# Attention scores as three float32r products of two halves, on the two halves of TensorE's rows

## The chip, the cores and the metric

The kernel runs on one core of one Trainium2 chip. The metric is device time in microseconds (us) of one execution, the median over the runs. The engines are TensorE (PE for its matmuls, PEld for its weight loads), VectorE (DVE), ScalarE (ACT) and GpSimd (POOL); the DMA transfers of this kernel are issued from SyncE's queue (SP).

## The reference, cut to what matters

Attention over 8 batches with 8 heads, 576 tokens and 64 numbers a head, and a gated layer on what it gives:

```
scores = scale * q @ k.T                       # [8, 8, 576, 576]
keep   = scores >= max(scores, axis=-1) - tau
attn   = softmax(where(keep, scores, -1e9))
x      = (attn @ v), heads side by side        # [4608, 512]
out    = (sigmoid(x @ w_gate) * (x @ w_val)) @ w_out   # d_ff = 1536
```

All inputs are float32.

## The kernel before, in words

**Staging.** A program in two layers runs on one core. The attention layer goes through 32 visits, one for each batch and each pair of heads. A visit has nine tiles of 128 queries: four of the first head, four of the second, and one "leftover" tile with the last 64 queries of both heads (its names have an `l`). For a tile, `tile_steps` computes 128x576 scores into PSUM (buffer `s`, two banks of 288 columns, two buffers in turn, L609), DVE takes the maximum (L616), the threshold is made from it (L625), ACT takes the exponential into SBUF (`p`, L630), and DVE zeroes what is below the threshold and sums (L633). A group of one or two tiles is then normalised on POOL (L667), transposed on TensorE (`tp`, L678; `lk` for the last 64 keys, L691), copied out (L640, L641), and multiplied with v (`av`, L714).

The second layer has products with 512 moving columns (`m` for the two input weights, L774; `o` for the output weights, L817). Three blocks of 512 tokens, batches 0 to 2, go this way during the attention. The other six blocks run after the last visit, two at a time, as seven products in place of eight (L1016, L1081; `two_blocks`), with sums of weights (`sums`, L868) made on POOL before.

**How scores are computed.** For the first four visits (`plain_s`, batch 0) scores are float32 matmuls: the stationary operand has 128 rows, of which one head's are non-zero (the input `q0` holds q so), the moving operand is k of both heads, in two halves of 288 keys. In the other 28 visits each float32 number is a sum of two float32r numbers, hi and lo. ACT makes hi of k and q (L529, L531), POOL makes lo of k (L533), DVE lo of q (L536), each for both heads at once, 640 columns. Then DMAs within SBUF lay the halves out anew: for each head, `qd` holds hi of q in one half of the partitions and lo in the other (L546), and `kd` holds hi of k in both halves of the partitions, and lo of k in both (L550). A matmul with 128 rows then gives hi·hi + lo·hi, and a second one hi·lo + lo·lo; with two halves of the keys a tile takes four matmuls with 128 rows and 288 moving columns. The leftover tile of such a visit takes six, from the tiles `q2` and `k2` that were not laid out anew.

**What sets the order.** Every step is given to `plan.op` with an engine, a cost, a key (lower goes first) and the buffers that it reads and writes. `Plan.run` walks a clock with these costs and emits each engine's instructions in the order that it finds. Attention tiles have keys that count up over the visits (`first`); a visit's loads and splits come `LEAD` tiles ahead; conversions of the weights have keys from `CONV_IN` and `CONV_OUT`; `SHIFT` is added to the keys of the visits from batch 1 on; matmuls of the second layer have keys of 1e6 and up, so that they fill what attention leaves of TensorE. `SLOTS` says how many buffers a tag has. `THR_UNTIL` and `LK_UNTIL` say up to which key the threshold is made on POOL instead of DVE, and the copy of `lk` on ACT instead of DVE. `SUMS_IN` and `SUMS_OUT` say in which block the sums of weights are made. The buffers of `two_blocks` come, in part, from tags that attention uses.

Of the kernel before, what the change touches and what calls it, by code (L numbers as in the profile page):

```python
# [43 lines left out]
class Plan:  # L44
# [3 lines left out]
    IN_TURN = ("x", "xf", "kn", "qn", "vn", "k2", "q2", "kd", "qd", "vs", "p", "pt", "pl", "ptc")  # L48
# [151 lines left out]
    "kn": 1, "qn": 1, "vn": 1, "k2": 1, "q2": 1, "kd": 3, "qd": 3, "vs": 3,  # L200
# [3 lines left out]
LEAD = 3  # L204
# [7 lines left out]
EARLY = 16  # L212
# [4 lines left out]
NPS = 4  # L217
# [15 lines left out]
THR_FIRST, THR_UNTIL, LK_UNTIL = "POOL", 72, 72  # L233
# [11 lines left out]
SHIFT = 20  # L245
# [13 lines left out]
KD_COST = 1.2  # L259
# [3 lines left out]
SUMS_IN, SUMS_OUT, SUM_KEY = {1: (0,), 2: (1,)}, {0: (0,), 1: (1,)}, 400  # L263
# [25 lines left out]
def kernel(  # L289
# [3 lines left out]
    q0: bass.AP,  # L293
# [22 lines left out]
    B, NPAIR, P, SK = k.shape  # L316
# [15 lines left out]
    assert D == 64 and SL == 64 and SK == SM + 2 * SL and ND == NPAIR == NJ and B * SL == SM  # L332
# [152 lines left out]
    class Visit:  # L485


        def __init__(self, b, hp, kind, first):
            self.b, self.hp, self.kind, self.first = b, hp, kind, first

            self.plain_s = 4 * b + hp < NPS
            self.of_tiles = {}
            self.name = f"{b}_{hp}{kind}"
            self.c0, self.c1 = {"": (0, SM), "a": (0, SM // 2), "b": (SM // 2, SM)}[kind]
            g0, g1 = [(0, (0, 1)), (1, (0, 1))], [(0, (2, 3)), (1, (2, 3))]
            left = [(None, (NJ,))]
            self.groups = {"": g0[:1] + left + g1[:1] + g0[1:] + g1[1:], "a": g0, "b": left + g1}[kind]
            self.with_left = kind != "a"
# [4 lines left out]
        def prepare(self, lead):  # L503
            key, n = self.first - lead, self.name
            b, hp = self.b, self.hp
            self.xf = buf("xf", [P, S], F32, f"xf{n}")
            if self.plain_s:
                self.plain_scores(key, n)
            else:
                self.split_scores(key, n)  # L510
# [4 lines left out]
        def split_scores(self, key, n):  # L515
            b, hp = self.b, self.hp

            kn = buf("kn", [P, SK], F32, f"kn{n}")
            op("SP", 1.2, key - 4, lambda: nc.sync.dma_start(out=kn.ap, in_=k[b, hp]), writes=[kn])


            c0, c1 = self.c0, self.c1 + (2 * SL if self.with_left else 0)
            W, WM = c1 - c0, self.c1 - self.c0
            qn = buf("qn", [P, W], F32, f"qn{n}")
            op("SP", 1.2, key - 4, lambda: nc.sync.dma_start(out=qn.ap, in_=q[b, hp, :, c0:c1]), writes=[qn])


            k2 = self.k2 = buf("k2", [P, 2, SK + P], F32R, f"k2{n}")
            op("ACT", 0.73, key, lambda: nc.scalar.copy(k2.ap[:, 0, :SK], kn.ap), reads=[kn], writes=[(k2, 0)])  # L529
            q2 = self.q2 = buf("q2", [P, 2, W], F32R, f"q2{n}")  # L530
            op("ACT", act(W), key, lambda: nc.scalar.activation(q2.ap[:, 0], qn.ap, AF.Copy, scale=scale_t[:, 0:1]),  # L531
               reads=[qn], writes=[(q2, 0)])
            op("POOL", pool(SK), key, lambda: nc.gpsimd.tensor_tensor(  # L533
                out=k2.ap[:, 1, :SK], in0=kn.ap, in1=f32(k2.ap[:, 0, :SK]), op=ALU.subtract
            ), reads=[kn, (k2, 0)], writes=[(k2, 1)])
            op("DVE", 1.4 * W / 640, key, lambda: nc.vector.scalar_tensor_tensor(  # L536
                out=q2.ap[:, 1], in0=qn.ap, scalar=scale_t[:, 0:1], in1=f32(q2.ap[:, 0]), op0=ALU.mult, op1=ALU.subtract
            ), reads=[qn, (q2, 0)], writes=[(q2, 1)])
            self.WM = WM
            self.kd, self.qd = {}, {}  # L540
            for h in range(2):
                kd = self.kd[h] = buf("kd", [P, 2, SK], F32R, f"kd{n}_{h}")
                qd = self.qd[h] = buf("qd", [P, WM], F32R, f"qd{n}_{h}")
                own, other = slice(h * D, (h + 1) * D), slice((1 - h) * D, (2 - h) * D)
                for z, rows in enumerate((own, other)):
                    op("SP", 0.5, key + h, lambda qd=qd, rows=rows, own=own, z=z: nc.sync.dma_start(  # L546
                        out=f32(qd.ap[rows]), in_=f32(q2.ap[own, z, :WM])
                    ), reads=[(q2, z)], writes=[(qd, z)])
                for rows in (own, other):
                    op("SP", KD_COST, key + h, lambda kd=kd, rows=rows, own=own: nc.sync.dma_start(  # L550
                        out=f32(kd.ap[rows]), in_=f32(k2.ap[own, :, :SK])
                    ), reads=[k2], writes=[(kd, rows.start)])

        def plain_scores(self, key, n):
            b, hp, c0, c1 = self.b, self.hp, self.c0, self.c1
            WM = self.WM = c1 - c0
            kn = self.k1 = buf(("kn", "qn")[hp % 2], [P, SK], F32, f"kp{n}")
            op("SP", 1.2, key - 4, lambda: nc.sync.dma_start(out=kn.ap, in_=k[b, hp]), writes=[kn])
            W = 2 * WM + (2 * SL if self.with_left else 0)
            qn = self.q1 = buf("kd", [P, W], F32, f"qp{n}")  # L560

            heads = [(0,), (1,)] if n == "0_0" else [(0, 1)]
            for hs in heads:
                c = slice(hs[0] * WM, (hs[-1] + 1) * WM)
                op("SP", 0.9 * len(hs), key - 4, lambda hs=hs, c=c: nc.sync.dma_start(
                    out=qn.ap[:, c].rearrange("p (h c) -> p h c", h=len(hs)),
                    in_=q0[4 * b + hp, :, hs[0] : hs[-1] + 1, c0:c1],
                ), writes=[(qn, h) for h in hs])
            if self.with_left:
                op("SP", 0.3, key - 4, lambda: nc.sync.dma_start(out=qn.ap[:, 2 * WM :], in_=q[b, hp, :, SM:]),  # L570
                   writes=[(qn, 2)])
            if len(heads) == 1:
                op("ACT", act(W), key, lambda: nc.scalar.activation(qn.ap, qn.ap, AF.Copy, scale=scale_t[:, 0:1]), writes=[qn])
                return
            for i, c in enumerate((slice(0, WM), slice(WM, 2 * WM), slice(2 * WM, W))):
                op("ACT", act(c.stop - c.start), key, lambda c=c: nc.scalar.activation(
                    qn.ap[:, c], qn.ap[:, c], AF.Copy, scale=scale_t[:, 0:1]
                ), writes=[(qn, i)])

    def tile_steps(vis, g, i, key):  # L580
# [8 lines left out]
        cols = None if h is None else slice(qt * P - vis.c0, (qt + 1) * P - vis.c0)  # L589
        if vis.plain_s:  # L590
            at = 2 * vis.WM if h is None else h * vis.WM + cols.start
            steps = [(lambda: vis.q1.ap[:, at : at + P], lambda c: vis.k1.ap[:, c])]
            reads = [(vis.q1, 2 if h is None else h), vis.k1]
        elif h is None:
            steps = [
                (lambda a=a: vis.q2.ap[:, a, vis.WM :], lambda c, z=z: vis.k2.ap[:, z, c])
                for a, z in ((0, 0), (0, 1), (1, 0))
            ]
            reads = [vis.q2, vis.k2]
        else:  # L600
            steps = [
                (lambda: vis.qd[h].ap[:, cols], lambda c, z=z: vis.kd[h].ap[:, z, c]) for z in range(2)
            ]
            reads = [vis.qd[h], vis.kd[h]]

        def scores():
            for m, (st, mv) in enumerate(steps):
                for c in range(2):
                    nc.tensor.matmul(  # L609
                        s.ap[:, c, :HALF], st(), mv(slice(k0 + c * HALF, k0 + (c + 1) * HALF)),  # L610
                        start=m == 0, stop=m == len(steps) - 1,
                    )

        op("PE", 0.98 if vis.plain_s else len(steps) * 2 * mm(HALF), key, scores, reads=reads, writes=[s], also=[g.p])
# [480 lines left out]
    def two_blocks(k):  # L1095

        key = 400 + k
        tags = ["x"] * 5 + ["vs"] * 2 + ["k2"] + ["kd"] * 3 + ["p"] * 3
        whole = lambda b: Part(b, lambda: b.ap)
        xt, j = {}, 0  # L1100
        for prod in SEVEN:
            xt[prod] = []
            for c in range(2):
                xt[prod].append(whole(buf(tags[j], [P, 2, SM], F32R, f"xs{k}_{prod}_{c}")))
                j += 1
# [111 lines left out]
    plan.run()  # L1217


_INS = ["q", "q0", "k", "v", "tau", "moe_w_gate", "moe_w_val", "moe_w_out"]  # L1220
_OUTS = [((512, 4608), "float32")]


# [73 lines left out]
```

## Time and profile before

| what | value |
|---|---|
| median of 3 runs | 1374.51 us (1374.49 to 1381.02) |
| the profiled execution's own time | 1375.02 us |
| its span, first to last instruction | 1373.2 us |
| mean granted TensorE clock | 0.995 |
| busy: PE, PEld, DVE | 1332.4, 1099.7, 982.3 us |
| busy: ACT, POOL | 708.8, 639.0 us |
| DMA | 317.70 MB, 231 GB/s |

The span and the profiled execution's own time differ by 1.8 us. Busy times are unions over a group of instructions; a matmul's record is longer than the step to the next one, since matmuls are pipelined, so the price of a tile of matmuls is read from the starts in the timeline: from its first start to the first start of what follows. A float32 matmul (`kp`,`qp` and `av`) has two records in the trace, a float32r matmul and a transpose one. L-numbers are lines of the kernel.

### The profile page before, as it was taken

Reading aid. Unit: us, or ns where it says so; the run is one execution under the profiler, and the core shown is the slowest. Engines: PE = TensorE matmul, PEld = TensorE weight load, DVE = VectorE, ACT = ScalarE, POOL = GpSimd, SP = SyncE. Lnnn points to the kernel's source line nnn. Section 1 sums busy time; section 2 is a strip of 40 time slices with the busy share of each in tenths; the row PEclk is TensorE's granted clock in tenths of the full one; section 3 lists DMA queues with packets and bytes.
Section 4 is the critical chain, followed back from the end, with each engine's and each line's share of the span. In section 5 each row is a group of like instructions: output and inputs, shape, how many; then the busy total and the mean of one; then the engine's idle time right before and its main releaser. Section 6 shows DMA issues by size and latency. Waiting matters only on the chain.

```text
span 1373.2 us, 23632 instructions
## 1 busy us (share of the span) xinstructions
PE 1332.4 (97%) x8276; PEld 1099.7 (80%) x8276; DVE 982.3 (72%) x2070; ACT 708.8 (52%) x1225; POOL 639.0 (47%) x681
## 2 busy tenths in 40 slices
PE   6888999999999999999999999999999999999998
PEld 5666888888788788888888887888888888888887
DVE  5898888777778787777878783456974569745584
ACT  5776766665566666566667663222532225322242
POOL 4888865884676685686787653011000110001100
PEclk9899999999999999999999999999999999999999
DMA  5769899888688779798879677766686566766664
GB/s 214 284 218 326 286 256 272 266 242 255 206 238 245 200 226 285 203 297 246 238 221 275 208 210 260 234 184 193 208 288 215 185 194 209 245 194 187 195 208 140
DMA packets 140292, 317.70 MB, mean 231 GB/s; under 512 B 22032, under 2 KB 49168, under 8 KB 140176
## 3 DMA queue, kind: packets, MB, share of 16 engines
q1 hardware_dynamic: 140032, 316.20, 75.0%
q8 instruction: 67, 1.10, 0.3%
q14 instruction: 49, 0.40, 0.1%
q10 hardware_dynamic: 144, 0.00, 0.0%
HBM read 210.24 MB, written 54.53 MB: 193 GB/s over the span
## 4 chain that ended last, share of the span: by engine, by line
PE 88%; DMA 4%; DVE 3%; issue 2%; POOL 2%; ACT 1%; SPq 0%; POOLq 0%; ACTq 0%; DVEq 0%
PE m L774 13%; PE qb L1016 11%; PE av L714 11%; PE s L609 10%; PE tp L678 7%; PE qc L1016 7%; PE qa L1016 7%; PE o L817 6%; PE rb L1081 5%; PE rc L1081 4%; PE ra L1081 4%; PE s_l L609 2%; DVE p L633 1%; PE tp_l L678 1%; PE lk L691 1%
## 5 line engine op out<-in xcount | busy, mean ns | idle before, releaser
L667 POOL TENSOR_SCALAR p<-p,zero_t,sm 128x576 f32<-128x576 f32 x256 | 215.1, 850 | 101.6 <-DVE sm L665 61.7
L616 DVE TENSOR_REDUCE st<-s 128x1 f32<-128x576 f32 x256 | 192.8, 754 | 84.0 <-PE s L609 82.6
L630 ACT ACTIVATE p<-s,st 128x576 f32<-128x576 f32 x256 | 190.5, 748 | 66.8 <-DVE st L616 56.3
L633 DVE SCALAR_TENSOR_TENSOR p<-s,st,p 128x576 f32<-128x576 f32 x256 | 206.4, 811 | 25.2 <-ACT p L630 19.0
L929 POOL TENSOR_TENSOR gA<-gA 128x512 f32<-128x512 f32 x18 | 24.2, 1343 | 417.1 <-DVE gA L995 417.1
L640 ACT COPY pt<-tp 128x512 f32<-128x512 f32 x256 | 148.6, 587 | 74.4 <-PE tp L678 73.4
L678 PE MATMUL tp<-ident,p 128*128 128x128 f32 x1024 | 157.0, 278 | 8.4 <-POOL p L667 8.1
L609 PE MATMUL s<-kd,qd 128*128 128x288 f32 x896 | 161.6, 305 | 3.5 <-DMA qd<-q 2.4
L774 PE MATMUL m<-x,wi 128*128 128x512 f32 x576 | 161.5, 405 | 0.0
L678 PEld LDWEIGHTS tp<-ident,p 128*128 128x128 f32 x1024 | 123.3, 142 | 34.6 <-POOL p L667 13.2
L609 PEld LDWEIGHTS s<-kd,qd 128*128 128x128 f32 x896 | 133.8, 189 | 14.4 <-DMA qd<-q 2.9
L714 PE MATMUL av<-pt,vs 128*64 128x256 f32 x1024 | 126.3, 385 | 0.7 <-ACT pt L640 0.7
L817 PE MATMUL o<-g,wo 128*128 128x512 f32 x432 | 120.1, 404 | 0.0
L953 DVE TENSOR_TENSOR qu<-qb,qp 128x512 f32<-128x512 f32 x72 | 49.8, 692 | 92.2 <-PE qb L1016 66.1
L774 PEld LDWEIGHTS m<-x,wi 128*128 128x128 f32 x576 | 98.8, 189 | 13.6
L1016 PE MATMUL qa<-xs_p,wa 128*128 128x512 f32 x432 | 109.6, 389 | 0.0
L714 PEld LDWEIGHTS av<-pt,vs 128*64 128x64 f32 x1024 | 68.4, 136 | 48.5 <-issue 7.7
L1016 PEld LDWEIGHTS qa<-xs_p,wa 128*128 128x128 f32 x432 | 81.1, 188 | 16.8
L817 PEld LDWEIGHTS o<-g,wo 128*128 128x128 f32 x432 | 74.5, 189 | 10.5
L921 ACT CAST gs_p<-gA 128x512 fp32r<-128x512 f32 x54 | 32.7, 620 | 77.4 <-DVE gA L995 41.5
L991 ACT ACTIVATE gA<-qa 128x512 f32<-128x512 f32 x18 | 10.8, 598 | 103.4 <-PE qa L1016 103.4
L640 ACT COPY xf<-av 128x256 f32<-128x256 f32 x64 | 25.6, 399 | 74.1 <-PE av L714 70.7
(151 smaller groups left out, 2687.5 us busy)
## 6 DMA issues: line engine op xcount, KB each, us to landing
kd<-k SPq DMA_DIRECT2D x112, 320.0 KB, 4.9
wi<-wid SPq DMA_DIRECT2D x48, 512.0 KB, 7.4
wo<-wod SPq DMA_DIRECT2D x36, 512.0 KB, 6.9
wa<-wid SPq DMA_DIRECT2D x36, 512.0 KB, 3.3
ws<-sid SPq DMA_DIRECT2D x36, 512.0 KB, 4.4
wt<-sid SPq DMA_DIRECT2D x36, 512.0 KB, 3.3
wo_p<-sod SPq DMA_DIRECT2D x36, 512.0 KB, 4.5
qd<-q SPq DMA_DIRECT2D x112, 128.0 KB, 3.4
```

Source lines behind the costliest of these rows:

```text
L609: nc.tensor.matmul(s.ap[:, c, :HALF], st(), mv(slice(k0 + c * HALF, k0 + (c + 1) * HALF)), start=m == 0, stop=m == len(steps) - 1,)
L616: op("DVE", 0.76, key, lambda: nc.vector.tensor_reduce(out=st.ap[:, 0:1], in_=sv(), axis=AX.XY, op=ALU.max, negate=True), reads=[s], write ...
L630: op("ACT", 0.74, key, lambda: nc.scalar.activation(p(), sv(), AF.Exp, bias=st.ap[:, 0:1], scale=1.0), reads=[s, (st, 0)], writes=[(g.p, i)])
L633: op("DVE", 0.9, key, lambda: nc.vector.scalar_tensor_tensor(out=p(), in0=sv(), scalar=st.ap[:, 1:2], in1=p(), op0=ALU.is_ge, op1=ALU.mult ...
L640: return op("ACT", act(n), key, lambda: nc.scalar.copy(dst(), src.ap), reads=[src], writes=[part])
L667: op("POOL", 0.9, key, lambda i=i: nc.gpsimd.tensor_scalar(out=p.ap[:, i * S : (i + 1) * S], in0=p.ap[:, i * S : (i + 1) * S], scalar1=zer ...
L678: nc.tensor.matmul(tp.ap[:, c, :], self.p.ap[:, o + c * P : o + (c + 1) * P], ident, is_transpose=True, start=c == 0, stop=c == NJ - 1, sk ...
L714: nc.tensor.matmul(av.ap[h * D : (h + 1) * D, a:z], vis.vs.ap[:, j, h], m(h), start=i == 0, stop=i == len(ms) - 1, skip_group_check=True,)
L774: nc.tensor.matmul(m.ap, wv[:, a, c * P : (c + 1) * P], xs[c].ap[:, z, c0:c1], start=e == 0, stop=e == 11,)
L817: nc.tensor.matmul(acc.ap, wv[:, f, a], g[fg * ND + f].ap[:, z], start=(fg, f, a, z) == (0, 0, 0, 0), stop=(fg, f, a, z) == (NFG - 1, ND - ...
L1016: nc.tensor.matmul(acc.ap, wv[:, y, (2 * h + c) * P : (2 * h + c + 1) * P], xt[prod][c].get()[:, z], start=e == 0 and prod in FIRST, stop= ...
L1081: nc.tensor.matmul(acc.ap, w.ap[:, e, c, y], gt[prod][2 * g + c].get()[:, z], start=m == 0 and g == 0 and prod in FIRST, stop=m == 5 and g ...
```

## The change

q and k now arrive with each head's 64 numbers twice: rows 0 to 63 and rows 64 to 127 of `q` both hold q of a head; of `k`, rows 0 to 63 hold the first half of the keys (352 columns, with an overlap) and rows 64 to 127 the second half. Heads lie side by side in the free dimension. A tile's matmul of one half of the keys uses 64 rows of TensorE, that of the other half the other 64 rows, and each writes its own bank of `s`. There are three products (hi·hi, hi·lo, lo·hi; lo·lo is left out), so six matmuls with 64 rows and 288 columns for a tile. The four plain visits use two float32 matmuls with 64 rows a tile in place of two with 128. The leftover tile is float32 in all visits, as four matmuls with 64 rows and 64 stationary columns (two heads by two halves), from the unsplit `kr` and a scaled copy `ql` of the last queries. `kd`, `qd`, `k2`, `q2` and the DMAs within SBUF are gone. The splits are made for each head apart: ACT two of 512 and two of 352 columns, POOL two of 352, DVE two of 512 in a visit.

The planner's numbers change too: `LEAD` 3 to 6, `SHIFT` 20 to 6, `LK_UNTIL` 72 to 108, `SUMS_OUT` from one quarter each in blocks 0 and 1 to both in block 1, and the slots; `two_blocks` takes its buffers from the new tags.

```diff
-    "kn": 1, "qn": 1, "vn": 1, "k2": 1, "q2": 1, "kd": 3, "qd": 3, "vs": 3,
+    "k": 2, "q": 2, "kr": 2, "qr": 1, "ql": 2, "vs": 3,
-LEAD = 3
+LEAD = 6
-THR_FIRST, THR_UNTIL, LK_UNTIL = "POOL", 72, 72
+THR_FIRST, THR_UNTIL, LK_UNTIL = "POOL", 72, 108
-SHIFT = 20
+SHIFT = 6
-SUMS_IN, SUMS_OUT, SUM_KEY = {1: (0,), 2: (1,)}, {0: (0,), 1: (1,)}, 400
+SUMS_IN, SUMS_OUT, SUM_KEY = {1: (0,), 2: (1,)}, {1: (0,1)}, 400
...
+            for h in range(2):
+                op("ACT", act(N), key + h, lambda h=h: nc.scalar.activation(
+                    qt.ap[:, 0, h], qr.ap[:, 0, h, :N], AF.Copy, scale=scale_t[:, 0:1]
+                ), reads=[] if qr is qt else [(qr, h)], writes=[(qt, h)])
+                if self.plain_s:
+                    continue
+                op("ACT", act(SK), key + h, lambda h=h: nc.scalar.copy(kt.ap[:, 0, h], kr.ap[:, 0, h, :SK]),
+                   reads=[(kr, h)], writes=[(kt, h)])
+                op("POOL", pool(SK), key + h, lambda h=h: nc.gpsimd.tensor_tensor(
+                    out=kt.ap[:, 1, h], in0=kr.ap[:, 0, h, :SK], in1=f32(kt.ap[:, 0, h]), op=ALU.subtract
+                ), reads=[(kr, h)], writes=[(kt, h)])
+                op("DVE", 1.4 * SM / 640, key + h, lambda h=h: nc.vector.scalar_tensor_tensor(
+                    out=qt.ap[:, 1, h], in0=qr.ap[:, 0, h, :SM], scalar=scale_t[:, 0:1], in1=f32(qt.ap[:, 0, h]),
+                    op0=ALU.mult, op1=ALU.subtract
+                ), reads=[(qr, h)], writes=[(qt, h)])
...
+        plain = vis.plain_s or h is None
+        steps = [(0, 0)] if plain else [(0, 0), (0, 1), (1, 0)]
+
+        heads = [(h, qt * P, 0, P)]
+        tq, tk = vis.qt, vis.kt
+        if h is None:
+            tq, tk = vis.ql, vis.kl
+            c0 = 0 if tq is not vis.qt else SM
+            heads = [(0, c0, 0, SL), (1, c0, SL, P)]
         def scores():
-            for m, (st, mv) in enumerate(steps):
-                for c in range(2):
-                    nc.tensor.matmul(
-                        s.ap[:, c, :HALF], st(), mv(slice(k0 + c * HALF, k0 + (c + 1) * HALF)),
-                        start=m == 0, stop=m == len(steps) - 1,
-                    )
+            for m, (a, z) in enumerate(steps):
+                for x, c0, r0, r1 in heads:
+                    for c in range(2):
+                        rows = slice(c * D, (c + 1) * D)
+                        nc.tensor.matmul(
+                            s.ap[r0:r1, c, :HALF], tq.ap[rows, a, x, c0 : c0 + r1 - r0],
+                            tk.ap[rows, z, x, k0 : k0 + HALF],
+                            start=m == 0, stop=m == len(steps) - 1, skip_group_check=True,
+                        )
```

On TensorE, around the last tiles of batch 1's fourth visit (`s1_3_120` is batch 1, pair 3, head 1, tile 2, first of its group; `m0_10_1` is a product of block 0), there stands before:

```order
L678 MATMUL tp1_3_020_2833<-ident_71,p1_3_02_2736 128x128 x4
L609 MATMUL s1_3_120_2839<-kd1_3_1_2366,qd1_3_1_2351 128x288 x4
L678 MATMUL tp1_3_021_2846<-ident_71,p1_3_02_2736 128x128 x4
L691 MATMUL lk1_3_02_2854<-ident_71,p1_3_02_2736 128x128
L609 MATMUL s1_3_121_2857<-kd1_3_1_2366,qd1_3_1_2351 128x288 x4
L774 MATMUL m0_10_1_0_2802<-x0_3_1393,wi0_10_1a_2550 128x512 x2
L774 MATMUL m0_11_0_0_2871<-x0_0_554,wi0_11_0a_2696 128x512 x2
```

And now, on the same engine and for the same tiles:

```order
L641 MATMUL tp1_3_020_2795<-ident_71,p1_3_02_2716 128x128 x4
L641 MATMUL tp1_3_021_2801<-ident_71,p1_3_02_2716 128x128 x4
L737 MATMUL m0_9_1_0_2671<-x0_2_1105,wi0_9_1a_2442 128x512
L737 MATMUL m0_9_1_0_2671<-x0_3_1385,wi0_9_1a_2442 128x512 x3
L654 MATMUL lk1_3_02_2816<-ident_71,p1_3_02_2716 128x128
L570 MATMUL s1_3_120_2820<-k1_3_2134,q1_3_2129 128x288 x6
L570 MATMUL s1_3_121_2830<-k1_3_2134,q1_3_2129 128x288 x6
```

The score tiles have six matmuls in place of four and read `k` and `q` straight; they still stand singly or in twos among transposes and products of the second layer, and the second layer's product beside them is an earlier one. Over the whole program a run of score tiles with 64 rows begins after another kind of matmul some 240 times.

On SP's queue, before, in batch 1 (`kn`, `qn` are loads from HBM, `qd`, `kd` the transfers within SBUF, `wi` and `wod` the second layer's weights):

```order
L519 DMA kn1_3_1967<-in_k_dram 128x640
L550 DMA kd1_2_0_1971<-k21_2_1905 64x2x640 x2
L546 DMA qd1_2_0_1984<-q21_2_1969 64x512
L513 DMA vs1_3_1992<-in_v_dram 128x768
L1187 DMA xp2_0_138<-xf1_0_1872 256x1x32
```

And now, in the same batch:

```order
L520 DMA qr1_3_1825<-in_q_dram 128x1152
L518 DMA kr1_3_1852<-in_k_dram 128x2x352
L477 DMA wod0_127<-ws0_2_1732 512x1x256
L504 DMA vs1_3_1922<-in_v_dram 128x768
L1156 DMA xp2_0_138<-xf1_0_1837 256x1x32
```

What is left of a visit's transfers on this queue are the loads of q, k and v, in larger pieces; nothing on it waits any more for a split to be made.

More of the change, by code (lines that the diff above doesn't have):

```diff
@@ L209, in POOL_MAX @@
     return True
-EARLY = 16
+EARLY = 12
 AHEAD = 4
@@ L292 @@
     q: bass.AP,
-    q0: bass.AP,
     k: bass.AP,
@@ L314 @@
     nc = tc.nc
-    B, NPAIR, P, SK = k.shape
+    B, NPAIR, P, _, SK = k.shape
     D = v.shape[-1]
@@ L506, in prepare, with load_scores @@
             self.xf = buf("xf", [P, S], F32, f"xf{n}")
[L507 to L510, printed above, removed]
+            self.load_scores(key, n)
             self.vs = buf("vs", [P, NJ + 2, 2, D], F32, f"vs{n}")
             op("SP", 1.2, key - 3, lambda: nc.sync.dma_start(out=self.vs.ap, in_=v[b, hp]), writes=[self.vs])
-        def split_scores(self, key, n):
+        def load_scores(self, key, n):
             b, hp = self.b, self.hp
[L518 to L540, printed above, removed]
-            for h in range(2):
[L542 to L578, printed above, removed]
@@ new lines, in load_scores @@
+            N = qt.shape[-1]
+            self.kl, self.ql = kr, qt
+            if not self.plain_s:
+                ql = self.ql = buf("ql", [P, 1, 2, SL], F32, f"ql{n}")
+                op("ACT", 0.3, key, lambda: nc.scalar.activation(
+                    ql.ap[:, 0], qr.ap[:, 0, :, SM:], AF.Copy, scale=scale_t[:, 0:1]
+                ), reads=[qr], writes=[ql])
+            for h in range(2):
+                op("ACT", act(N), key + h, lambda h=h: nc.scalar.activation(
[12 more added lines that the diff above has]
+                ), reads=[(qr, h)], writes=[(qt, h)])
@@ L1097, in two_blocks, with places @@
         key = 400 + k
-        tags = ["x"] * 5 + ["vs"] * 2 + ["k2"] + ["kd"] * 3 + ["p"] * 3
         whole = lambda b: Part(b, lambda: b.ap)
[L1100 to L1105, printed above, removed]
-        base = {}
-        tags = iter(["qd"] * 3 + ["kn", "qn", "vn"] + ["xf"] * 2)
+        def places(tag, n, name, shape=(2, SM), dtype=F32R):
+            two = NPS < B * NPAIR and tag in "qk" or tag in ("x", "qr") and dtype is F32
+            bs = [buf(tag, [P, 2, *shape] if two else [P, *shape], dtype, f"{name}_{tag}{i}") for i in range(0, n, 1 + two)]
+            if not two:
+                return [whole(b) for b in bs]
+            return [Part(b, lambda b=b, i=i: b.ap[:, i], i) for b in bs for i in range(2)][:n]
+        base, at = {}, []
+        for tag, n in (("k", 4), ("xf", 2), ("x" if NPS == B * NPAIR else "qr", 2)):
+            at += places(tag, n, f"xb{k}", (SM,), F32)
         for hp in (0, 2, 1, 3):
             for z in range(2):
-                b = buf(next(tags), [P, SM], F32, f"xb{k}_{hp}_{z}")
-                op("SP", 1.0, key, lambda b=b, hp=hp, z=z: nc.sync.dma_start(
-                    out=b.ap, in_=xp_d[k][hp].t[:, z].rearrange("p b s -> p (b s)")
-                ), reads=[xp_d[k][hp]], writes=[b])
-                base[hp, z] = whole(b)
+                x = base[hp, z] = at.pop(0)
+                op("SP", 1.0, key, lambda x=x, hp=hp, z=z: nc.sync.dma_start(
+                    out=x.get(), in_=xp_d[k][hp].t[:, z].rearrange("p b s -> p (b s)")
+                ), reads=[xp_d[k][hp]], writes=[(x.b, x.part)])
+        xt = {}
+        for tag, n in (("x", 5), ("vs", 3), ("q", 3), ("p", 3)):
+            at += places(tag, n, f"xs{k}")
+        for prod in SEVEN:
+            xt[prod] = [at.pop(0) for c in range(2)]
         for c in range(2):
@@ L1124, in two_blocks @@
             if j % 2:
-                bs = [buf(("kd", "p")[i // 3], [P, 2, SM], F32R, f"gs{n}_{i}") for i in range(6)]
-                gt[prod] = [whole(b) for b in bs]
+                gt[prod] = places("q", 3, f"gs{n}") + places("p", 3, f"gs{n}")
             else:
@@ L1129, in two_blocks @@
                 gt[prod] = [Part(b, lambda b=b, i=i: b.ap[:, i], i) for b in bs for i in range(2)]
-                gt[prod] += [whole(buf(t, [P, 2, SM], F32R, f"gs{n}_{t}")) for t in ("q2", "ptc")]
+                gt[prod] += places("w", 1, f"gs{n}") + places("ptc", 1, f"gs{n}")
         for i, f in enumerate(F1):
@@ L1135, in two_blocks @@
         out_two(k, gt)
-    visits = [(b, hp, "") for b in range(B) for hp in range(NPAIR)]
+    visits = [(b, hp) for b in range(B) for hp in range(NPAIR)]
     t = 0
     todo = []
-    for b, hp, kind in visits:
+    for b, hp in visits:
         if b == 1 and hp == 0:
             t += SHIFT
-        vis = Visit(b, hp, kind, t)
+        vis = Visit(b, hp, t)
         t += vis.n_tiles()
```

64 lines of the change are left out of this document (24 added, 40 removed).

## The prediction

> **What bounds the kernel now.** I read the busy time by stage first, then the chain of waits, the groups of the score matmuls, and the timeline around a few score tiles. The first view gives, for each stretch, the length and then the busy time of PE, PEld, DVE, ACT and POOL, the granted clock, the DMA share and GB/s.
>
> ```profile
> 0.00:120.00 120.00, 93.49 (x556) 67.27 (x558) 97.05 (x199) 82.82 (x153) 84.21 (x123) 0.94 0.72 248
> 120.00:830.00 710.00, 699.55 (x5301) 586.51 (x5299) 552.24 (x1375) 458.12 (x783) 499.66 (x518) 1.00 0.84 246
> 830.00:1373.00 543.00, 539.38 (x2423) 445.98 (x2419) 333.00 (x497) 167.90 (x289) 55.10 (x42) 1.00 0.65 209
> ```
>
> The next two rows are the chain of work that ended last, by engine and by line.
>
> ```profile
> PE 88%; DMA 4%; DVE 3%; issue 2%; POOL 2%; ACT 1%; SPq 0%; POOLq 0%; ACTq 0%; DVEq 0%
> PE m L774 13%; PE qb L1016 11%; PE av L714 11%; PE s L609 10%; PE tp L678 7%; PE qc L1016 7%; PE qa L1016 7%; PE o L817 6%; PE rb L1081 5%; PE rc L1081 4%; PE ra L1081 4%; PE s_l L609 2%; DVE p L633 1%; PE tp_l L678 1%; PE lk L691 1%
> ```
>
> From 120 to 830 us (28 visits and the filling products) PE idles 10.5 of 710 us, while DVE is busy for 78%, POOL 70%, ACT 65%: TensorE sets the pace there, and what a score tile costs it is worth that much. In the first 120 us (the four plain visits and conversions) PE idles 26.5 us and DVE is busy for 81%: a chain through both. After 830 us no score is computed.
>
> **The float32r tile.** Its price now, and that of its neighbours (first column the start in us):
>
> ```profile
> 407.76 0.69 PE L609 MATMUL s<-kd,qd 128*128 128x288 f32 x4
> 408.29 1.54 PE L774 MATMUL m<-x,wi 128*128 128x512 f32 x6
> 409.66 0.69 PE L609 MATMUL s<-kd,qd 128*128 128x288 f32 x4
> 410.19 2.90 PE L774 MATMUL m<-x,wi 128*128 128x512 f32 x12
> 412.93 0.49 PE L678 MATMUL tp<-ident,p 128*128 128x128 f32 x3
> ```
>
> From start to start a tile of four takes 0.53 us, 0.1325 a matmul; twelve products of 512 columns take 2.74, 0.228 each. The changed tile has six matmuls of 288 columns in three pairs. If a pair's halves run side by side it takes 3 x 0.1325 = 0.40 us, 0.13 less; if not, 0.80. No matmul here uses 64 rows, but `av` uses the array in two halves of 64 columns:
>
> ```profile
> 398.43 1.03 PE L609 MATMUL s_l<-k,q 128*128 128x288 f32 x6
> 399.31 0.63 PE L774 MATMUL m<-x,wi 128*128 128x512 f32 x2
> 399.87 1.95 PE L714 MATMUL av<-pt,vs 128*64 128x256 f32 x16
> 401.64 0.61 PE L714 MATMUL av<-pl,vs 128*64 128x128 f32 x8
> 402.08 0.63 PE L714 MATMUL av<-pt_l,vs 128*64 128x64 f32 x16
> 402.54 0.29 PE L714 MATMUL av<-pl_l,vs 128*64 128x64 f32 x4
> 402.76 0.80 PE L609 MATMUL s<-kd,qd 128*128 128x288 f32 x4
> 403.40 0.60 PE L678 MATMUL tp<-ident,p 128*128 128x128 f32 x4
> 403.75 0.77 PE L609 MATMUL s<-kd,qd 128*128 128x288 f32 x4
> 404.37 0.60 PE L678 MATMUL tp<-ident,p 128*128 128x128 f32 x4
> 404.80 0.27 PE L691 MATMUL lk<-ident,p 128*128 128x128 f32 x1
> ...
> 171.17 0.29 PE L714 MATMUL av<-pl_l,vs 128*64 128x64 f32 x4
> 171.39 0.66 PE L678 MATMUL tp<-ident,p 128*128 128x128 f32 x4
> 171.80 0.77 PE L609 MATMUL s<-kd,qd 128*128 128x288 f32 x4
> ```
>
> Sixteen records with 256 columns start within 399.87 to 401.64: 0.111 us each. A 512-column product takes 0.228 alone, so 256 columns would take about 0.114 for one pass; these are float32 at two passes a record (a plain tile below: 0.97 for four records of 288, 0.24 each, nearly twice 0.1325). So two halves do run side by side. The weights keep up too: sixteen loads of 64 columns fit in 402.08 to 402.54, 2,200 columns a microsecond, by which the two 128-column loads of a new pair need 0.115, under 0.1325.
>
> The price of going into this mode and out of it stands in the same rows. In: two products should take 0.456 and take 0.56 (399.31 to 399.87), 0.10 more. Out: the last four records should take 0.115 at the rate of the sixteen before, and take 0.22; the score tile behind them takes 0.64 instead of 0.53 (in the second excerpt the transposes behind take 0.41, against 0.43 from 404.37 to 404.80). Together 0.20 to 0.31 us a visit to the mode. The changed program enters the 64-row mode some 240 times, so this unknown decides the sign. Its bounds are 0, as between transposes and float32r products (another format, the same shape of the array: four transposes and a score tile take 403.40 to 404.37, 0.97, which is the 0.43 of the next four and 0.54), and 0.31, as with `av`. I take 0.04. Halves by rows share neither the partitions that they read nor a bank that they write, and each 128-column output stays whole, while `av` splits the output columns: it is the output side that is new in `av` and not here. That is a reason, not a row, and the rival below is its price if it fails.
>
> [...]
>
> How many tiles there are, and what else the change replaces, stands in the groups (count, then busy us and mean ns of one, then idle time before them and what ended it):
>
> ```profile
> L609 PE MATMUL s<-kd,qd 128*128 128x288 f32 x896 | 161.6, 305 | 3.5 <-DMA qd<-q 2.4 <-DVE p L633 1.1
> L609 PE MATMUL s<-kp,qp 128*128 128x288 f32 x128 | 43.4, 479 | 19.4 <-DVE p L633 14.3 <-ACT qp L576 3.3 <-PE lk L691 0.9
> L609 PE MATMUL s_l<-k,q 128*128 128x288 f32 x168 | 29.0, 308 | 0.0
> L536 DVE SCALAR_TENSOR_TENSOR q<-qn,scale_t,q 128x640 fp32r<-128x640 f32 x28 | 32.2, 1151 | 1.8 <-ACT q L531 0.5
> L529 ACT CAST k<-kn 128x640 fp32r<-128x640 f32 x28 | 20.4, 728 | 3.8 <-PE s_l L609 3.2 <-DMA wi<-wid 0.3 <-DMA sod<-s_o 0.2
> L531 ACT ACTIVATE q<-qn,scale_t 128x640 fp32r<-128x640 f32 x28 | 23.3, 833 | 1.1 <-DMA qd<-q 1.1
> L533 POOL TENSOR_TENSOR k<-kn,k 128x640 fp32r<-128x640 f32 x28 | 45.5, 1624 | 14.8 <-ACT k L529 12.7 <-issue 2.2
> L641 DVE COPY pl<-lk 128x128 f32<-128x128 f32 x104 | 29.7, 286 | 19.0 <-PE lk L691 18.4
> L625 POOL TENSOR_SCALAR st<-st,ntau_t 128x1 f32<-128x1 f32 x48 | 12.7, 267 | 22.3 <-DVE st L616 21.9
> ```
>
> So a float32r tile goes from 0.53 to 0.44, and 896 records by four are 224 tiles: 224 x 0.09 = **20 us less**, between 29 less (0) and 40 more (0.31).
>
> Two plain tiles in the timeline, the first a leftover tile:
>
> ```profile
> 40.43 1.14 PE L609 MATMUL s_l<-kp,qp 128*128 128x288 f32 x4
> 41.40 1.13 PE L609 MATMUL s<-kp,qp 128*128 128x288 f32 x4
> ```
>
> **The leftover tiles.** 168 records by six are 28 tiles, six at 0.1325 = 0.80 us each. Now they are one float32 pass over four quarters of the array, half of a plain tile's 0.97 (40.43 to 41.40): 0.485. They do split the columns, so they pay the 0.25 of `av`: 0.735, 28 x 0.065 = **2 less** (9 less without a price).
>
> **The plain tiles.** 36 tiles go from 0.97 to 0.485 + 0.04. In a stage where PE idles anyway, the shorter tile only shortens the chain score, maximum, exponential, threshold; DVE at 81% gives back part. I count half: 36 x 0.445 / 2 = **8 less** (0 to 17).
>
> **The DMAs.** The transfers within SBUF by count, size and us to landing:
>
> ```profile
> kd<-k SPq DMA_DIRECT2D x112, 320.0 KB, 4.9
> qd<-q SPq DMA_DIRECT2D x112, 128.0 KB, 3.4
> ```
>
> 112 transfers of 320 KB and 112 of 128 KB go, some 50 of 317.70 MB; the doubled loads bring less than a fifth of that back. The price of their wait is small: the groups show 2.4 us of PE idle ended by `qd`, the first split visit's. **2 less.** `LEAD` 6 and `SHIFT` 6 move loads and splits ahead of tiles and past weight loads on SP's queue; SP no longer holds a weight load behind a copy that waits for a split. I put nothing on it.
>
> **The splits.** By columns, DVE's two of 512 take 1.84 against 1.15 us a visit, ACT's two and two with the scaled last queries about 2.5 against 1.56, POOL's two of 352 1.8 against 1.62. Later thresholds by `first` (`SHIFT` makes keys smaller) move 30 copies of `lk` (0.286) from DVE to ACT and 18 threshold steps to POOL (0.267 each). Over 28 visits DVE gets some 8 us more, ACT 32, POOL 10. With a stage some 25 us shorter, DVE is at 82%, POOL 74%, ACT 72%: hidden behind PE, but score buffers are released a little later now and then. **2 more** (0 to 10). If this cover were gone, the 8 us of DVE would be the price. `SUMS_OUT` moves POOL's sums of output weights wholly into block 1; they are needed after 830 us, where POOL is busy for 10%: nothing.
>
> Sum: -20 - 2 - 8 - 2 + 2 = -30 on the profiled execution's 1375.0 us (its span of 1373.2 and 1.8 around it): 1345. The median of the runs is 0.5 lower, so I predict **1344.5 us**. Runs of this kernel lie up to 0.5% apart (1374.49 to 1381.02), which is what a measurement can tell from no change.
>
> **The rivals.**
>
> *A: each change of mode is paid, by rows as by columns.* [...] At 0.25 a tile takes 0.65, 224 x 0.12 = 27 more; leftover tiles 2 less, plain ones 18 x (0.97 - 0.735) = 4 less, the rest cancels: 1375 + 21 = 1396 (1384 at 0.20, 1410 at 0.31). It decides for slower from about 0.165 a tile. For it: the only rows with another shape of the array show 0.20 to 0.31. Against: the argument on the output side, and formats that change for nothing. [...] Chance 0.18.
>
> *B: the halves do not run side by side.* Then 224 x 0.27 = 60 more, leftover tiles 28 x (1.94 - 0.80) = 32 more, plain tiles nothing: 1467. Against it: the pairs of `av`. Chance 0.03.
>
> *C: TensorE gets free and nothing uses it.* With shorter score tiles the attention chain through DVE (four steps a tile) sets the pace from 120 us on, and PE idles instead; only the first stage's 8 and the 2 remain: about 1366. For it: DVE gets more work. Against: 82% is no bound, and the second layer's products can fill. Chance 0.07.
>
> **How the numbers follow.** Forecast 0.72, A 0.18, B 0.03, C 0.07. The forecast's own range comes from the bounds: lowest -29 - 9 - 17 - 2 = -57, 1318; highest 1376, where a change of mode costs 0.165. That holds C and the forecast, and leaves out A and B, some 2 in 10. Faster by over 0.5%: the forecast but for 0.03, and half of C: 0.73. Slower: A but for 0.02, and B: 0.19. Within 0.5%: 0.08.
>
> **What would show it.** The timeline after: score tiles of six whose start-to-start step to the next product is about 0.44 us. 0.60 to 0.71 is A, 0.80 is B; steps as forecast with PE idle of much more than 10 us between 120 and 800 is C. A leftover tile near 0.5 instead of 0.73 would say that quarters change mode for nothing. The attention should end some 25 to 30 us earlier, the stage after it take its 543 us as before; DMA bytes should fall by about 40 MB. If that stage differs by over 5 us, the sum missed something in `two_blocks`.

## The result, and the profile after

The changed kernel is slower: 1412.19 us median (1410.15 to 1413.71, 4 runs) against 1376.93 for the kernel before, ratio 1.0252 with a 95% interval of 1.0219 to 1.0286. Its profiled execution has a span of 1411.9 us, 38.7 more than the profile before. The busy times by stage, in the columns of the prediction's first view:

```profile
0.00:120.00 120.00, 91.44 (x642) 58.68 (x642) 101.78 (x205) 86.90 (x165) 89.47 (x129) 0.84 0.72 253
120.00:830.00 710.00, 706.33 (x5417) 510.24 (x5415) 529.32 (x1259) 465.26 (x845) 487.28 (x537) 1.00 0.55 180
830.00:1373.00 543.00, 540.76 (x2589) 440.45 (x2586) 346.87 (x560) 182.87 (x316) 75.26 (x62) 1.00 0.62 201
```

Between 120 and 830 us PE idles less than before (3.7 us instead of 10.5), DVE, POOL and the DMAs are busy for less, and yet less gets done: all of it is TensorE's own time. Two rows give the stages: where the second layer's first product starts, and where the paired blocks start. In the timeline of the kernel before, first column the start in us:

```profile
123.52 2.44 PE L774 MATMUL m<-x,ws 128*128 128x512 f32 x10
...
855.14 1.52 PE L1016 MATMUL qa<-xs_p,wa 128*128 128x512 f32 x6
```

And in that of the changed kernel:

```profile
114.01 2.33 PE L737 MATMUL m<-x,ws 128*128 128x512 f32 x9
...
890.10 2.88 PE L979 MATMUL qa<-xs_x,wa 128*128 128x512 f32 x12
```

So the plain visits end 9.5 us earlier (114.0 against 123.5), the filling stage takes 776.1 us instead of 731.6, 44.5 more, and what follows 521.8 instead of 518.1, 3.7 more. The sum is the 38.7. The timeline shows what a score tile costs in that stage:

```profile
410.14 0.65 PE L641 MATMUL tp<-ident,p 128*128 128x128 f32 x4
410.63 0.27 PE L654 MATMUL lk<-ident,p 128*128 128x128 f32 x1
410.83 0.67 PE L570 MATMUL s<-k,q 64*128 64x288 f32 x6
411.43 0.73 PE L737 MATMUL m<-x,wi 128*128 128x512 f32 x2
411.99 0.60 PE L641 MATMUL tp_l<-ident,p_l 128*128 128x128 f32 x4
```

The tile itself takes 0.60 us to the next start, but its neighbours grow too: one transpose (`lk`, 0.108 by the four in 0.43 of before) takes 0.20, two products (0.456) take 0.56. From 410.63 to 411.99 it is 1.36 us for work that should take 0.108 + 0.40 + 0.456 = 0.96: a stay in the 64-row shape (one entry, the tiles done there, and the way back) costs 0.40 us, and the tile with its stay 0.80 instead of 0.53. This tile is no exception: over the 186 single tiles of the trace that stand between transposes and products of the full shape with no idle time, the stay costs 0.395 us in the median and 0.383 in the mean, beyond 0.1325 a pair, 0.229 a product and 0.1085 a transpose. The weight loads of the same stretch show where that goes:

```profile
410.52 0.14 PEld L654 LDWEIGHTS lk<-ident,p 128*128 128x128 f32 x1
410.83 0.43 PEld L570 LDWEIGHTS s<-k,q 64*128 64x128 f32 x6 [0.17 <-issue]
411.43 0.30 PEld L737 LDWEIGHTS m<-x,wi 128*128 128x128 f32 x2 [0.16 <-issue]
411.76 0.59 PEld L641 LDWEIGHTS tp_l<-ident,p_l 128*128 128x128 f32 x4
```

PEld stands idle for 0.17 and 0.16 us, waiting for nothing that the profile shows, ahead of the first load on either side of the tile; the loads of `tp_l`, where the shape stays, start 0.23 us ahead of their matmuls (411.76 against 411.99). At both changes of shape in these rows the first load is not made ahead: it starts with the matmuls that need it (410.83 and 411.43 in both views). The waits of PEld over the whole run (us in total, times, longest) say the same. Before, those that nothing in the profile explains were these ahead of score tiles and transposes, and none ahead of the products `m`:

```profile
PEld s L609 <- issue: 11.7, 7, 2.8
PEld tp L678 <- issue: 4.5, 25, 0.3
```

After:

```profile
PEld s L570 <- issue: 49.7, 153, 2.6
PEld tp L641 <- issue: 21.2, 91, 0.8
PEld m L737 <- issue: 16.8, 93, 0.4
```

### The profile page after: what moved, and what is told of

It is laid out like the page before. It is cut to its first block, busy times and chain, and to the rows that moved or that the text cites. A ratio compares the mean times of both kernels' runs of the same rounds, so it can differ in the third digit from the quotient of the medians.

```text
span 1411.9 us, 24265 instructions
## 1 busy us (share of the span) xinstructions
PE 1373.6 (97%) x8796; PEld 1038.1 (74%) x8796; DVE 995.8 (71%) x2050; ACT 745.1 (53%) x1341; POOL 652.0 (46%) x727
## 2 busy tenths in 40 slices
DMA packets 118742, 274.74 MB, mean 195 GB/s; under 512 B 18400, under 2 KB 53216, under 8 KB 118624
## 5 line engine op out<-in xcount | busy, mean ns | idle before, releaser
L570 PE MATMUL s<-k,q 64*128 64x288 f32 x1472 | 177.6, 347 | 20.0 <-DVE p L596 16.9
L570 PEld LDWEIGHTS s<-k,q 64*128 64x128 f32 x1472 | 109.7, 190 | 87.9 <-issue 49.7
L737 PE MATMUL m<-x,wi 128*128 128x512 f32 x576 | 167.4, 416 | 0.0
L641 PE MATMUL tp<-ident,p 128*128 128x128 f32 x1024 | 163.7, 286 | 3.2 <-POOL p L630 2.9
L641 PEld LDWEIGHTS tp<-ident,p 128*128 128x128 f32 x1024 | 119.5, 144 | 48.4 <-issue 21.2
L780 PE MATMUL o<-g,wo 128*128 128x512 f32 x432 | 128.6, 419 | 0.0
L924 ACT ACTIVATE qp<-qa 128x512 f32<-128x512 f32 x36 | 21.5, 597 | 83.9 <-PE qa L979 83.8
L537 POOL TENSOR_TENSOR k<-kr,k 128x352 fp32r<-128x352 f32 x56 | 55.1, 987 | 19.0 <-ACT k L535 18.7
L540 DVE SCALAR_TENSOR_TENSOR q<-qr,scale_t,q 128x512 fp32r<-128x512 f32 x56 | 58.4, 1043 | 0.0
L916 DVE TENSOR_TENSOR qu<-qc,qu 128x512 f32<-128x512 f32 x72 | 49.7, 691 | 11.4 <-PE qc L979 10.1
```

Source lines behind the costliest of these rows:

```text
L570: nc.tensor.matmul(s.ap[r0:r1, c, :HALF], tq.ap[rows, a, x, c0 : c0 + r1 - r0], tk.ap[rows, z, x, k0 : k0 + HALF], start=m == 0, stop=m == ...
L641: nc.tensor.matmul(tp.ap[:, c, :], self.p.ap[:, o + c * P : o + (c + 1) * P], ident, is_transpose=True, start=c == 0, stop=c == NJ - 1, sk ...
L737: nc.tensor.matmul(m.ap, wv[:, a, c * P : (c + 1) * P], xs[c].ap[:, z, c0:c1], start=e == 0, stop=e == 11,)
L780: nc.tensor.matmul(acc.ap, wv[:, f, a], g[fg * ND + f].ap[:, z], start=(fg, f, a, z) == (0, 0, 0, 0), stop=(fg, f, a, z) == (NFG - 1, ND - ...
```

## The experiments

Theory S says that each stay in the 64-row shape costs about 0.39 us, and that this is the loss. Rival N says that the planner's new numbers, or the larger splits, made a worse order; rival W that matmuls with 64 rows are slow by themselves.

**1. The shape undone, all else kept.** Each float32r tile of the changed kernel as four matmuls with 128 rows from the same buffers, in the same order:

```diff
+            if not plain:
+                for m in range(2):
+                    for c in range(2):
+                        nc.tensor.matmul(
+                            s.ap[:, c, :HALF], tq.ap[:, m, h, qt * P : qt * P + P], tk.ap[:, m, h, k0 : k0 + HALF],
+                            start=m == 0, stop=m == 1, skip_group_check=True,
+                        )
+                return
```

> The changed kernel, its loads, splits, numbers and order kept, but each float32r score tile is four matmuls with all 128 rows, straight from k and q (the scores are then sums over both halves of the keys, which leaves out the right scores). Theory S (each stay of TensorE in the 64-row shape costs about 0.39 us, read from the trace of after: 0.095 and 0.105 on the way in, 0.085 and 0.106 on the way out): a tile falls from about 0.80 with its neighbours to 0.53, the stage from 120 us on loses about 50 us: 1362 (1352 to 1372). Rival N (the new numbers put the work in a worse order), or the larger splits on DVE, ACT and POOL as the cause: it stays at 1405 to 1415.

Measured: 1363.01 us (1362.37 to 1364.38), ratio to before 0.9887 (0.9866 to 0.9909). The loss is gone and a gain of 16 us against the runs of the kernel before beside it stands in its place, with the change's loads, splits, numbers and order. By the same two starts as above, its stages take 112.9, 726.2 and 521.7 us, where the changed kernel's take 114.0, 776.1 and 521.8: nearly the whole difference lies in the filling stage, where the float32r tiles are. The same sequence of work in its timeline:

```profile
410.10 0.27 PE L662 MATMUL lk<-ident,p 128*128 128x128 f32 x1
410.12 0.77 PE L569 MATMUL s<-k,q 128*128 128x288 f32 x4
410.73 0.62 PE L745 MATMUL m<-x,wi 128*128 128x512 f32 x2
411.20 0.69 PE L569 MATMUL s<-k,q 128*128 128x288 f32 x4
```

From `lk` to the end of the two products it is 1.10 us, 0.108 + 0.53 + 0.456, with nothing on top.

**2. What the prediction counted on.** Three matmuls with 128 rows:

```diff
+                for m, c in ((0, 0), (0, 1), (1, 0)):
```

> As the one with four, but three matmuls with 128 rows a float32r tile (one half of the keys lacks a product): the 0.40 us without a switch that the prediction counted on. Theory S: another 224 x 0.13 = 29 us less, 1333 (1322 to 1345). If DVE or another engine takes over as the bound, it stays within 10 us of the one with four.

Measured: 1335.47 us (1334.84 to 1336.87), ratio 0.9686 (0.9669 to 0.9704).

```profile
406.46 0.27 PE L661 MATMUL lk<-ident,p 128*128 128x128 f32 x1
406.49 0.65 PE L568 MATMUL s<-k,q 128*128 128x288 f32 x3
406.98 0.63 PE L744 MATMUL m<-x,wi 128*128 128x512 f32 x2
407.44 0.60 PE L648 MATMUL tp_l<-ident,p_l 128*128 128x128 f32 x4
```

Here the sequence takes 0.98 us. TensorE still sets the pace at 43 us under before (PE is busy for 677.6 of the 680 us from 120 us on): no other engine takes over, so rival C of the prediction falls. From here to the changed kernel it is 76.7 us, all of it in the filling stage (699.2 us here). The changed kernel's 224 float32r tiles make 217 stays, 7 of them with two tiles, so a stay costs 0.35 us over the whole program. That is below 0.40: the mean single stay is 0.383, and 21 stays lie beside `av` or a leftover tile, which use a part of the array too (128*64 and 64*64 in the timeline), so that they border on the full array on one side only, or on none; that these cost less is inferred from the total, not measured.

**3. and 4. The shape entered twice a tile, and its control.** One small matmul with 128 rows between the first and second pair of each float32r tile; the control has the same one in the middle of each float32r tile of the kernel before.

```diff
+                if m == 0 and not plain:
+                    nc.tensor.matmul(s.ap[:, 0, SM - 16 :], ident, ident[:, :16], start=False, stop=False, skip_group_check=True)
```

> The changed kernel with one small float32 matmul of 128 rows and 16 columns between the first and the second pair of each float32r tile, into columns of the bank that nothing reads: each tile goes into the 64-row shape twice. Theory S: 0.39 us more a tile and the small matmul itself (0.05 to 0.2): 224 x 0.44 to 0.59, 1510 to 1545. Rival W (the 64-row matmuls are slow by themselves, the change of shape costs little): 10 to 45 us more, 1422 to 1457.

> The control for the run that goes into the shape twice: the same small matmul in the middle of each float32r tile of the kernel before, where no shape changes. Both theories: only the small matmul itself, 224 x 0.05 to 0.2 us, 1388 to 1422.

Measured: 1533.83 and 1415.82 us, one run each, beside 1378.95 for the kernel before. The small matmul alone costs 36.9 us, 0.165 a tile; in the changed kernel it costs 121.6, 0.543 a tile. The second stay is the difference, 0.38 us; the kernel before spread over 6 us in these runs, which is 0.03 a tile. The tile in the timeline of the first of these:

```profile
450.04 0.27 PE L656 MATMUL lk<-ident,p 128*128 128x128 f32 x1
450.25 0.40 PE L570 MATMUL s<-k,q 64*128 64x288 f32 x2
450.57 0.40 PE L576 MATMUL s<-ident 128*128 128x16 f32 x2
450.90 0.53 PE L570 MATMUL s<-k,q 64*128 64x288 f32 x4
451.36 1.19 PE L739 MATMUL m<-x,wi 128*128 128x512 f32 x4
```

One pair takes 0.32 to the next start, and a small matmul of 16 columns 0.33, when both sides of each are a change of shape; two pairs together take 0.46. Rival W falls: the pairs are fast, the changes are not.

**5. The numbers alone.** In the kernel before (`LEAD` and the slots, which change too, stay as they were):

```diff
-THR_FIRST, THR_UNTIL, LK_UNTIL = "POOL", 72, 72
+THR_FIRST, THR_UNTIL, LK_UNTIL = "POOL", 72, 108
-SHIFT = 20
+SHIFT = 6
-SUMS_IN, SUMS_OUT, SUM_KEY = {1: (0,), 2: (1,)}, {0: (0,), 1: (1,)}, 400
+SUMS_IN, SUMS_OUT, SUM_KEY = {1: (0,), 2: (1,)}, {1: (0,1)}, 400
```

> The kernel before with SHIFT 6, LK_UNTIL 108 and SUMS_OUT of the change alone. Theory S: the planner's numbers are no cause of the loss; 1365 to 1380 (part of what the kernel with four full matmuls gained over before may be theirs). Rival N (the new numbers put the work in a worse order): 1395 or more.

Measured: 1384.69 us (1382.02 to 1388.17), ratio 1.0045 (1.0015 to 1.0074): some 6 us slower, 5 above the top of what S expected, and less than a fifth of the loss. The gain of the first experiment is not theirs.

**6. Both tiles of a group in one step.** Meant to halve the number of stays:

```diff
+        if i == 0:
+            g.ss = [buf("s", [P, 2, SM], F32, f"s{g.name}{j}") for j in range(g.n)]
+        s = g.ss[i]
```

> The changed kernel with the score tiles of a group of two put in one step, so that both follow each other on TensorE and some 90 of about 205 stays in the 64-row shape go. Theory S (the price is paid by the stay): 90 x 0.39 = 35 us less than 1412, so 1377 (1370 to 1392, since the step now needs both score buffers free). If the price is paid by the tile: 1405 to 1425.

Measured: 1499.97 us (1499.16 to 1501.57), ratio 1.089. The expectation missed by 120 us, and the total tells nothing on the price of a stay. The edit built a new wait: a step needs both score buffers free, so TensorE and DVE take turns (this is read from the waits below and was not tested by a run of its own). The stretch before the last attention products, and the waits over the attention stage:

```profile
750.00:970.00 220.00, 169.99 (x1374) 124.69 (x1374) 150.43 (x389) 115.75 (x204) 79.87 (x90) 0.83 0.21 64
```

```profile
DVE st L582 <- PE s L572: 146.9, 96, 3.8
```

DVE waits 147 us for scores (113.8 in the changed kernel), the attention falls behind, the filling products run out, and PE idles 50 of the 220 us, at a granted clock of 0.83. The timeline still tells what the total does not, namely that the price goes by the stay and not by the tile:

```profile
505.50 1.06 PE L572 MATMUL s<-k,q 64*128 64x288 f32 x12
506.49 1.19 PE L783 MATMUL o<-g,wo 128*128 128x512 f32 x4
```

Two tiles in one stay take 0.99 us to the next start, where a tile alone takes 0.60. In the changed kernel the 7 stays with two tiles cost 0.40 us in the median, as much as those with one.

**7. 128 rows, nothing copied within SBUF.** q and k come twice, hi is made in all partitions, lo of q in the second half only; `k` and `q` have three buffers in place of two, `kr` one in place of two:

```diff
+                            s.ap[:, c, :HALF], tq.ap[:, 0, h, qt * P : qt * P + P],
+                            vis.kh[h].ap[:, m, k0 + c * HALF : k0 + (c + 1) * HALF],
...
+                    out=qt.ap[D:, 0, h], in0=qr.ap[D:, 0, h, :SM], scalar=scale_t[D:, 0:1], in1=f32(qt.ap[D:, 0, h]),
```

> A kernel with the reference's outputs, float32r tiles with all 128 rows as before (hi and lo of q stacked, four products) but nothing copied within SBUF: q and k come twice, in both halves of the partitions, hi is made in all of them, lo of q only in the second half, lo of k in both. Plain and leftover tiles and the numbers as in the change. Theory S: as the kernel with four full matmuls, 1363, or up to 10 us more since POOL and ACT make 640 columns of k for each head (1358 to 1375). If the copies within SBUF had been what the change must keep for another reason, or POOL becomes the bound: over 1380.

Measured: 1374.14 us (1370.69 to 1378.49), ratio 0.9979 (0.9959 to 1.0): at the upper end of S's range, 11 us above the first experiment. Its plain tiles are those of the change, which alone bring 7 us (experiment 8). That the copies go is therefore worth nothing that these runs could show, once their work is paid on POOL and ACT.

**8. The plain tiles alone.** In the kernel before:

```diff
+            if vis.plain_s:
+                for x, a0, r0, r1 in heads:
+                    for c in range(2):
+                        rows = slice(c * D, (c + 1) * D)
+                        nc.tensor.matmul(
+                            s.ap[r0:r1, c, :HALF], vis.q1.ap[rows, x, a0 : a0 + r1 - r0], vis.k1.ap[rows, x, k0 : k0 + HALF],
+                            start=True, stop=True, skip_group_check=True,
+                        )
+                return
```

> The kernel before with the change's plain tiles alone (two float32 matmuls with 64 rows a tile, the four-quarter leftover tile, their own inputs), all else as before. Both after and the kernels with full matmuls start the second layer at 113 to 114 us, before and e1_numbers at 124 to 125. If the plain tiles are the cause, as theory S has it (0.485 and 0.39 are still under 0.97, in a stage where the chain counts): second layer from about 114 us, 10 us less in all, 1368 (1362 to 1373). If it is the earlier loads (LEAD) or the order: 1373 to 1383.

Measured: 1372.08 us (1363.81 to 1379.40), ratio 0.9951 (0.993 to 0.9971), 7 us less: the one version with the reference's outputs whose interval lies wholly below the kernel before. The second layer starts here:

```profile
116.81 1.30 PE L610 MATMUL s<-kd,qd 128*128 128x288 f32 x4 [2.43 <-DMA qd<-q]
117.91 2.33 PE L775 MATMUL m<-x,ws 128*128 128x512 f32 x5
```

That is 5.6 us earlier than before, and 3.9 later than in the changed kernel and than expected; 2.4 of the 3.9 are the wait for the copy `qd`, which the change removes.

**9. The planner told the price.** The changed kernel with 0.80 us for every score tile in place of 0.44 and 0.57.

> The changed kernel with the planner's cost of every score tile at 0.80 us, about what a tile and its two changes of shape take in the trace of after, instead of 0.44 and 0.57. Theory S: the price stays, only the order shifts, 1400 to 1420. Rival N (the order made from too low a price is the loss): under 1395.

Measured: 1406.73 us (1405.81 to 1407.28), ratio 1.02 (1.0174 to 1.0225). Some 5 us of the loss (7 by the ratios, whose intervals just touch) may come from the order that the low price led to; the rest stays, so rival N explains a small part at most.

**10. Old numbers in the kernel without copies.** The seventh kernel with `SHIFT` 20, `LK_UNTIL` 72 and `SUMS_OUT` as before.

> The kernel with full matmuls and no copies within SBUF, but SHIFT 20, LK_UNTIL 72 and SUMS_OUT as in the kernel before (LEAD 6 and the slots kept). The new numbers alone cost the kernel before 6 us (ratio 1.0045, 1.0015 to 1.0074); if they cost this one as much, 1374 less 6: 1368 (1364 to 1372), under both kernels. If they only suit another order: 1372 to 1380.

Measured: 1378.13 us (1376.40 to 1381.83), ratio 0.9991 (0.9977 to 1.0005): 4 us above the seventh kernel's, but their ratios to the kernel before (0.9991 and 0.9979) have intervals that overlap. The 6 us that the new numbers cost in the fifth experiment are not won back here by the old ones, so they cannot be carried over to another kernel.

## Why the prediction was wrong

**The step that failed** is "I take 0.04" for a change of shape. It is 0.38 to 0.40 a stay (timeline, and experiments 3 and 4; 0.35 over the whole program by experiment 2), nine to ten times that, and above the upper bound of 0.31 too. At 0.40 the prediction's own sum for the tile is 0.40 + 0.40 instead of 0.53, 224 x 0.27 = 60 more instead of 20 less. Measured for the shape alone, all else equal, are 49.2 us (the changed kernel less experiment 1), since the mean stay costs a little less than 0.40 and some stays are shared or lie beside another part-array shape. The other terms of the sum came to 10 less; experiment 1, whose tile has its old price, shows 16 less.

The reason given was that rows halve the input side and `av` the output side. Nothing in the trace had shown that the output side is what costs, and it is not: the output columns are the same 128 in the changed kernel and in experiment 1, and only the first pays. The bound was low in part because `av` was read from grouped rows. In the records, the first step of a new shape is longer than the next ones: in the tile at 410.83, the first pair starts 0.24 us ahead of the second, the second 0.13 ahead of the third. In and out, the parts of the price are 0.095 before the tile, 0.105 in its first step, 0.085 before the next and 0.106 in that one's first step. For `av` the part in the first step was counted as streaming (the sixteen records in 1.77 us): in single records the first step at 399.87 takes 0.27 us and the following ones 0.22, so that `av` comes to about 0.36 a visit instead of 0.31. Why rows cost slightly more than that stays open.

**Rival A was right that rows pay about as columns do**: 0.38 to 0.40 us a stay, against about 0.36 a visit for `av`. Its price of 0.25 was too low. By the prediction's formula it put the point of no change at 0.165, and the time at 1384 to 1410, just under the 1412 measured. The trace also shows the next weights loaded in the open (PEld's 0.16 to 0.17 us of idle time, and loads that start with their matmuls). How much of the 0.4 us that exposed load makes up, and what makes up the rest, was not separated.

**Rival B was wrong.** The two halves do run side by side: the six matmuls of a tile take 0.60 us to the next start with both their waits, less than the 0.80 that six in turn would take without any, and in the single records the second half starts 3 ns behind the first. **Rival C was wrong**: in experiment 2 no other engine stops the gain.

**Leftover tiles**: 2 less was forecast. One takes 0.64 to the next start and its neighbours grow by 0.16, so 0.80, as before: nothing gained.

**Plain tiles**: 8 less was forecast, experiment 8 has 7 for them. The size was right by luck: they pay some 0.35 too, not 0.04. At the full clock such a tile (61.85 in the changed kernel) took 0.69 to the next start, and the transposes beside it grew by 0.15, so 0.84 in all, 0.35 above the estimated 0.485 of its matmuls and still under 0.97, in a stage where the chain counts; where the granted clock was 0.50 (47.56 to 48.82 in the changed kernel) such a tile took 1.26 us to the next start, against 0.69 at the full clock (36.99 to 37.68). **The DMA wait**: 2 less was forecast, the 2.43 in experiment 8's row is gone after. Bytes fell by 43 MB (317.70 to 274.74), as forecast.

**Splits**: DVE has 13.5 us more (8 forecast), ACT 36 (32), POOL 13 (10). DVE's is larger because the split of 512 columns takes 1.04 us in the mean, not 0.92 (in experiment 3's trace it does take 0.92; why the mean differs was not tried):

```profile
L540 DVE SCALAR_TENSOR_TENSOR q<-qr,scale_t,q 128x512 fp32r<-128x512 f32 x56 | 58.4, 1043 | 0.0
```

It was hidden, as said: PE idles only 3.7 of the 710 us. **After the attention** nothing was expected; it is 3.7 us longer. It is as long in experiments 1 and 2 (521.7 and 521.8), so the shape is not the cause. PE waits some 2 us there, and not at all before. The first inputs of the paired blocks are late, as block 2 ends 6 us after the last `av` instead of 18; two of the waits:

```profile
894.18 0.50 PE L979 MATMUL qc<-xs_x,ws 128*128 128x512 f32 x1 [0.51 <-ACT xs_x L884]
895.09 2.11 PE L979 MATMUL qc<-xs_x,ws 128*128 128x512 f32 x8 [0.41 <-DVE xs_x L887]
```

## What to carry to other kernels

In this kernel a matmul that uses half of TensorE's rows was cheap in company and dear alone (experiment 3: two pairs in one stay took 0.46 us to the next start, a pair alone 0.32). So ask how many stays in such a shape a program makes, and price each, with the 0.35 to 0.40 us of these runs as a first estimate, before counting the halves that run side by side. Here a stay cost that and saved some 0.13 us of streaming (0.53 to 0.40 a tile, by 0.1325 a matmul). Where the only rows that show a kind of switch give it a price, take that price as the likeliest, and read it from the time of the whole neighbourhood (what came before, the step, what comes after) against the same work without the switch, not from the gap alone.

## What the runs showed of the hardware that was not expected

Weights for another shape of the array are not loaded ahead in the rows shown: PEld stands idle for 0.16 to 0.17 us at the changes on both sides of the tile, while within one shape the loads of `tp_l` start 0.23 us ahead. A matmul of 16 columns in float32 costs 0.165 us among others of its shape (experiment 4's control). And the granted clock of the first 120 us fell from 0.94 to 0.84 in the changed kernel, with PE busy for 91.4 us instead of 93.5. In experiment 8, where the plain tiles alone are changed, it fell to 0.82 with PE busy for 93.9 us, so it came with these tiles and what was changed for them in both kernels; how much of what they save goes back by it was not measured. Whether it follows from PE's gaps or from the shape was not tried.
